# One core, three layers: a GpSimd subtraction cut in four, routed rows fetched two units ahead, first counts a step later

## The chip, the core and the metric

The kernel runs on one core of a Trainium2 chip. The metric is the device time of one execution in microseconds; less is better. TensorE multiplies matrices, VectorE and ScalarE work element by element and can read TensorE's accumulators (PSUM), GpSimd works element by element on SBUF only and issues indirect loads and stores, SyncE issues plain loads and stores.

## The reference, cut to what matters

A gated linear attention (an mLSTM, 4 batches, 8 heads, 768 positions, 40 features), then a dense layer pair with squared ReLU, then a mixture of 8 experts in which each of 3072 tokens goes to the one expert with the largest logit:

```
for t in range(S):                        # attention, per batch and head
    m_new = max(f[t] + m, i[t])
    C = exp(f[t] + m - m_new) * C + exp(i[t] - m_new) * outer(v[t], k[t])
    n = exp(f[t] + m - m_new) * n + exp(i[t] - m_new) * k[t]
    y[t] = sigmoid(o[t]) * (C @ q[t]) / max(abs(n @ q[t]), 1)
g = relu(x @ w_in) ** 2 ; x = g @ w_out   # dense, 320 -> 2048 -> 320
e = argmax(x @ w_gate, axis=1)            # routed, 320 -> 1024 -> 320
out[token] = gate * relu(x[token] @ w1[e]) @ w2[e]
```

All is in float32. The kernel multiplies in a faster format and therefore splits operands in a rounded high part and a low part (the value minus its high part).

## The kernel before, in words

**Attention and dense part.** The 3072 tokens are 24 chunks of 128, and a dense group is 3 chunks (8 groups). While TensorE runs the dense layers of group g, the attention of later chunks is woven in between in small steps; `attend` makes 0.7 half steps for each of a group's 16 pairs of first layer (`l1`, line 802) and second layer (`l2`, line 833). Two first layers run ahead of the second (`AHEAD`). All engines have queues that are worked off in order, in the order in which the program writes them.

From chunk 7 on (`WHOLE`) the operands of the scores are split. `round(j)` (line 614) does this for the keys (j = 0) and the queries (j = 1) of the next chunk: ScalarE writes the scaled and rounded copy into `kq` (line 619), GpSimd subtracts it from `st` in place over 1024 columns (line 620). That is 2 x 17 subtractions. Around them GpSimd adds a bias to the decays `Ab` (line 648), masks them (line 649), and weighs the values (line 664); ScalarE takes the exponential of `Ab` (line 654) after the mask. In the same ScalarE queue stand the activations of the dense layers, `g` and `gh` (lines 821, 822). VectorE then makes `g` squared again and its low part `gl` (lines 828, 829), which the second layer needs.

**A group's end.** `fin(g)` (line 915) is a generator; each `next` on it is one step, and one step is made in each of the following iterations of the second layer. It writes the group's rows, transposes them for the logits `lp`, and then works on VectorE: logits, largest value and its index, the index as a number (`ei`, line 946). For group 0 it also counts the tokens per expert: the one-hot rows `on` (line 950) are summed by three small matmuls `ep` (line 952), and the fullest expert is chosen to be the first one. Then follow the one-hot `oh` (line 967), the softmax's exponent on VectorE and ScalarE (969, 970), and, a step later, the ranks' matmuls `pr` (line 973).

**Routed part.** `routed_experts` has one program for each engine with counting semaphores. A unit is up to 384 tokens of one expert; between 7 and 15 units, all but the first with weights loaded by SyncE, split by ScalarE (high) and by VectorE and GpSimd (low; GpSimd has piece 5). For unit u+1 TensorE transposes the gathered rows (`xT`, line 260) in the middle of unit u, at steps 5 and 6 of its first layer and in its second. It waits there for the indirect loads on `sG`. GpSimd's body for unit t is: gather the rows of unit t+1 (three indirect loads), scatter the results of unit t-1, make low piece 5 of unit t+1, drain. `gather(u)` waits on `sXL` until the rows of unit u-2 are split, since it writes their buffer. Orders of the others that matter are written out:

```
ACT_ORDER = "g0 g1 h0 g2 g3 h1 g4 g5 h2 g6 g7 x0 x1 h3 x2 h4 h5 p0 p1 p2".split()
DVE_ORDER = "g0 g1 l0 g2 g3 l1 g4 g5 l2 g6 g7 x0 x1 l3 x2 l4".split()
```

g: first layer's output; h and l: high and low pieces of the next unit's weights; x: the next unit's rows; p: output.

Of the kernel before, what the change touches and what calls it, by code (L numbers as in the profile page):

```python
# [9 lines left out]
F32 = mybir.dt.float32  # L10
# [8 lines left out]
ALU = mybir.AluOpType  # L19
# [66 lines left out]
def routed_experts(tc, pools, weights, x_d, w12, out, idx, tab, c0, gts, ident):  # L86

    nc = tc.nc
# [7 lines left out]
    op = [ps.tile([128, DM], F32, name=f"op{i}") for i in range(2)]  # L96
# [6 lines left out]
    def cell(e, u, j, lo, hi):  # L103
        return e.value_load(tab[u:u + 1, j:j + 1], min_val=lo, max_val=hi)

    def first_weights(e, load, have):

        with e.If(cell(e, 0, 3, 0, 1) < 1):
            load()
        with e.Else():  # L110
            have()

    def nest(e, body):

        mine = bass.OrderedEngineSet([e.engine])
        name = lambda t, k="": f"{e.engine.name}_unit{t}{k}"
        for t in range(MIN - 1):
            body(t, True)
        n = cell(e, 0, 2, MIN, NU)
        e.br(name(MIN - 1))  # L120
        for t in range(MIN - 1, NU):
            if t < NU - 1:
                with nc.body(name(t), valid_engines=mine):
                    e.br_cond(n > t + 1, name(t, "more"), name(t, "last"))
                with nc.body(name(t, "more"), valid_engines=mine):
                    body(t, True)
                    e.br(name(t + 1))
            with nc.body(name(t, "last" if t < NU - 1 else ""), valid_engines=mine):
                hint = e.mark_branch_hint_location()
                body(t, False)  # L130
                e.br(name(NU)).branch_hint(hint)
        nc.switch_bb(name(NU))
# [17 lines left out]
    def low(e, u, j):  # L150
        e.wait_ge(sH[j], u + 1)
        o = wl[u % 2][0][:, cut[j]] if j < 3 else wl[u % 2][1][:, CUT[j] - W1:CUT[j + 1] - W1]
        e.tensor_tensor(out=o, in0=raw[:, cut[j]], in1=wh[u % 2][:, cut[j]].bitcast(F32), op=ALU.subtract).then_inc(sW[j], 1)

    def pool(e):
        def gather(u):
            if u >= 2:
                e.wait_ge(sXL, 3 * (u - 1))
            for j in range(3):
                i = 3 * (u % 2) + j  # L160
                e.indirect_dma_start(out=xg[u % 2][:, j], out_offset=None, in_=x_d, in_offset=bass.IndirectOffsetOnAxis(ap=idx[:, 3 * u + j:3 * u + j + 1].bitcast(U32), axis=0)).then_inc(sG[i], 16)  # L161

        def put(at, j):
            e.indirect_dma_start(out=out, out_offset=bass.IndirectOffsetOnAxis(ap=at.bitcast(U32), axis=0), in_=ot[j], in_offset=None, bounds_check=NT - 1, oob_is_err=False).then_inc(sO[j], 16)  # L164

        def scatter(u, js=range(3)):
            for j in js:
                e.wait_ge(sOT, 3 * u + j + 1)
                put(idx[:, 3 * u + j:3 * u + j + 1], j)

        def body(t, more):
            if t:
                gather(t + 1)
            if t:
                scatter(t - 1)
            if more:
                for j in POOL_LO:
                    low(e, t + 1, j)
                e.drain()  # L179
            else:  # L180
                c = cell(e, t, 0, 1, GT)
                scatter(t, [0])
                for j in (1, 2):
                    with e.If(c > L * j):
                        scatter(t, [j])
                        e.wait_ge(sO[j], 16 * (t + 2))
                    with e.Else():
                        e.wait_ge(sO[j], 16 * (t + 1))
                e.wait_ge(sO[0], 16 * (t + 2))
        gather(1)  # L190
        for j in range(3):
            put(idx0[:, j:j + 1], j)
        first_weights(e, lambda: [low(e, 0, j) for j in POOL_LO], lambda: [e.sem_inc(sW[j], 1) for j in POOL_LO])
        nest(e, body)

    def act(e):
# [169 lines left out]
def kernel(ctx, tc, qk, q3, kvo, gates, w_in, w_out, wg, w12, cst, out, dbg=None):  # L366
    nc = tc.nc
# [218 lines left out]
    class Chunk:  # L586
# [27 lines left out]
        def round(self, j):  # L614

            if j == 0:
                self.kq = at1.tile([120, 2, H * L], F32R, tag="kq", name="kq")
            o = self.kq[:, j]
            nc.scalar.activation(out=o, in_=self.st[j], func=ACTF.Copy, scale=third[:, j:j + 1])  # L619
            nc.gpsimd.tensor_tensor(out=o, in0=self.st[j], in1=o.bitcast(F32), op=ALU.subtract)  # L620

        def decays(self):
            self.Ab = []
# [223 lines left out]
    def bc(ap, n):  # L847
        return ap.to_broadcast([ap.shape[0], ap.shape[1], n])

    def row(ap, n):  # L850
        return ap.rearrange("p (o e) -> p o e", o=1).to_broadcast([ap.shape[0], n, ap.shape[1]])
# [35 lines left out]
    def counts(p, start, stop, *parts):  # L887

        for i, (cols, x) in enumerate(parts):
            nc.tensor.matmul(p[:, cols].rearrange("p t e -> p (t e)"), ones, x.rearrange("p t e -> p (t e)"), start=start and i == 0, stop=stop and i == len(parts) - 1)  # L890
# [24 lines left out]
    def fin(g, acc):  # L915
# [31 lines left out]
        if g == 0:  # L947

            on = rw.tile([128, 3, 8], BF16, tag="so", name="on")
            nc.vector.tensor_tensor(out=on, in0=row(io8, n), in1=bc(ei, 8), op=ALU.is_equal)  # L950
            ep = psa.tile([128, 1, 8], F32, tag="a", name="ep")
            counts(ep, True, True, *[(slice(0, 1), on[:, t:t + 1]) for t in range(n)])
            yield
            mc = rw.tile([128, 8], F32, tag="mc", name="mc")
            nc.vector.tensor_copy(out=mc, in_=ep[:, 0])
            mm = rw.tile([128, 8], F32, tag="mm", name="mm")
            nc.vector.max(out=mm, in_=mc)
            mi = rw.tile([128, 8], U32, tag="mi", name="mi")
            nc.vector.max_index(out=mi, in_max=mm, in_values=mc)
            ef = rw.tile([128, 1], F32, tag="ef", name="ef")  # L960
            nc.vector.tensor_copy(out=ef, in_=mi[:, 0:1])
            nc.vector.tensor_copy(out=e0, in_=ef[0:1])
            ri = rw.tile([128, 8], I32, tag="ri", name="ri")
            nc.vector.tensor_tensor(out=ri, in0=io8, in1=ef.to_broadcast([128, 8]), op=ALU.add)
            nc.vector.tensor_scalar(out=ri, in0=ri, scalar1=7, scalar2=None, op0=ALU.bitwise_and)
            nc.vector.tensor_copy(out=rot, in_=ri)
# [156 lines left out]
    with tc.manual_schedule():  # L1123
# [36 lines left out]
        def layer2():  # L1160
# [21 lines left out]
            if f == NF - 1:  # L1182
                if g == NG - 1:
                    for j in range(i - 2, i + 1):
                        l2(g, accs[g], [2], its[j][1], *gs.pop(j))
                q = fin(g, accs.pop(g))
                next(q)
                before = list(fins)
                fins.append(q)
                if g == NG - 2:  # L1190
                    leave(brief)
                    p0 = ctx.enter_context(tc.tile_pool(name="p0", bufs=1, side="right"))
                    w0.extend([p0.tile([128, WN], F32R, name="w0h"), p0.tile([128, W1], F32R, name="w01l")])
                    fins.append(first_unit(before, p0))
                if g == NG - 1:
                    leave(dense)
                    fins[:] = [last_tokens(q)]
# [136 lines left out]
        while nd[0] < len(its):  # L1334
            i = nd[0]
# [126 lines left out]
```

## Time and profile before

| what | us |
|---|---|
| median of 3 runs shown (816.49 to 826.73) | 817.44 |
| the profiled execution | 819.06 |
| its span | 817.3 |
| TensorE busy in it | 761.4 |
| VectorE / ScalarE / GpSimd busy | 532.6 / 434.7 / 356.5 |
| mean granted TensorE clock | 0.978 |

All rows below are of that profiled execution, in microseconds from the start of its span. The engines are PE (TensorE; PEld its weight loads), DVE (VectorE), ACT (ScalarE), POOL (GpSimd), SP (SyncE). The attention runs until about 470 us beside the dense part, the dense part until about 560, and the routed part from about 595 us.

### The profile page before, as it was taken

The numbers are of one execution on the slowest core, as the hardware profiler recorded it, in microseconds if no ns is written. First come the engines' busy times: TensorE is split into PE (matmuls) and PEld (weight loads), VectorE is DVE, ScalarE is ACT, GpSimd is POOL, SyncE is SP. The second block draws the span as 40 slices with busy tenths as digits, with TensorE's granted clock in tenths as the row PEclk, the third lists the DMA queues.
The fourth block names the chain that finished last, engine by engine and source line by source line (L and its number), as shares of the span: only waits on it lengthen the run. The fifth ranks groups of instructions, "written<-read, shape, count | busy, mean of one in ns | idle before, by whom it ended". The sixth has DMA issues, their size and how long they took to land.

```text
span 817.3 us, 14079 instructions
## 1 busy us (share of the span) xinstructions
PE 761.4 (93%) x5075; PEld 745.2 (91%) x5075; DVE 532.6 (65%) x1169; ACT 434.7 (53%) x810; POOL 356.5 (44%) x329
## 2 busy tenths in 40 slices
PE   5779989989989999999999999999989999799995
PEld 3679989989989999989998999999989999699995
DVE  5678787777686787776679755362556546667553
ACT  5788785534544643543454533553256555566553
POOL 3774665535552553463345300423125334556423
PEclk9999999989999999998999999999999999999998
DMA  7777536344834344334335000100167566577602
GB/s 202 191 233 219 162 118 167 110 141 120 250 105 127 111 116 134 107 105 140 107 115 160 8 1 30 32 30 1 60 231 253 173 194 187 185 225 222 193 24 60
DMA packets 58824, 109.30 MB, mean 134 GB/s; under 512 B 7132, under 2 KB 36413, under 8 KB 58614
## 3 DMA queue, kind: packets, MB, share of 16 engines
q1 hardware_dynamic: 49542, 84.67, 35.4%
q0 software_dynamic: 4160, 11.77, 5.0%
q10 hardware_dynamic: 5040, 11.82, 4.9%
q8 instruction: 46, 0.75, 0.4%
q14 instruction: 36, 0.29, 0.1%
HBM read 99.37 MB, written 10.50 MB: 134 GB/s over the span
## 4 chain that ended last, share of the span: by engine, by line
PE 47%; issue 19%; POOL 10%; DVE 8%; DMA 7%; ACT 4%; POOLq 3%; SPq 0%; ACTq 0%; DVEq 0%
PE hp L813 18%; PE acc L842 6%; PE acc L844 5%; PE acc L843 5%; DMA st<-in_qk_dram 5%; POOL out_dram L164 4%; PE pv L748 3%; POOLq L179 3%; PE sp L739 2%; PE tp L704 2%; PE lp L907 2%; POOL kq L620 1%; POOL xrl L161 1%; PE xpt L713 1%; DVE gl L829 1%
## 5 line engine op out<-in xcount | busy, mean ns | idle before, releaser
L842 PE MATMUL acc<-wo_h,gh 128*128 128x320 f32 x384 | 126.1, 328 | 0.0
L821 ACT ACTIVATE g<-hp 128x384 f32<-128x384 f32 x128 | 62.3, 487 | 114.2 <-PE hp L813 109.2
L844 PE MATMUL acc<-wo_h,gl 128*128 128x320 f32 x384 | 120.2, 313 | 0.9 <-DVE gl L829 0.9
L843 PE MATMUL acc<-wo_l,gh 128*128 128x320 f32 x384 | 119.7, 312 | 0.0
L620 POOL TENSOR_TENSOR kq<-st,kq 120x1024 fp32r<-120x1024 f32 x34 | 83.7, 2464 | 81.8 <-ACT kq L619 72.1
L813 PE MATMUL hp<-xh,win_h 128*128 128x384 f32 x384 | 115.1, 354 | 3.7 <-ACT scr L902 1.3
L828 DVE SCALAR_TENSOR_TENSOR g<-hp,g 128x384 f32<-128x384 f32 x128 | 70.3, 549 | 68.2 <-ACT gh L822 68.2
L829 DVE TENSOR_TENSOR gl<-g,gh 128x384 fp32r<-128x384 f32 x128 | 97.0, 758 | 8.2
L249 DVE SCALAR_TENSOR_TENSOR gl<-hp,gh 128x384 fp32r<-128x384 f32 x88 | 47.7, 555 | 78.5 <-ACT gh L219 77.1
L813 PE MATMUL hp<-xh,win_l 128*128 128x384 f32 x384 | 89.1, 340 | 0.0
L813 PE MATMUL hp<-xl,win_h 128*128 128x384 f32 x256 | 88.1, 344 | 0.0
L844 PEld LDWEIGHTS acc<-wo_h,gl 128*128 128x128 f32 x384 | 73.3, 191 | 1.2 <-DVE gl L829 1.2
L842 PEld LDWEIGHTS acc<-wo_h,gh 128*128 128x128 f32 x384 | 73.7, 192 | 0.4
L843 PEld LDWEIGHTS acc<-wo_l,gh 128*128 128x128 f32 x384 | 73.6, 192 | 0.0
L813 PEld LDWEIGHTS hp<-xh,win_h 128*128 128x128 f32 x384 | 66.9, 193 | 5.8 <-DVE Ab L743 2.1
L822 ACT ACTIVATE gh<-g 128x384 fp32r<-128x384 f32 x128 | 67.2, 525 | 8.6 <-PE acc L843 4.6
L813 PEld LDWEIGHTS hp<-xh,win_l 128*128 128x128 f32 x384 | 70.6, 192 | 0.0
L219 ACT ACTIVATE gh<-hp 128x384 fp32r<-128x384 f32 x88 | 42.9, 491 | 50.5 <-PE hp L280 50.0
L619 ACT ACTIVATE kq<-st,cs 120x1024 fp32r<-120x1024 f32 x34 | 39.0, 1146 | 50.6 <-DMA st<-in_qk_dram 44.0
L748 PEld LDWEIGHTS pv<-kvo,Ab 128*128 128x128 f32 x384 | 56.2, 219 | 9.2 <-DVE Ab L743 3.4
L748 PE MATMUL pv<-kvo,Ab 128*128 128x42 f32 x384 | 55.0, 301 | 7.9 <-DVE Ab L743 5.1
L648 POOL TENSOR_TENSOR Ab<-Ab,cT 128x512 f32<-128x512 f32 x46 | 56.2, 1222 | 0.2
(265 smaller groups left out, 1848.7 us busy)
## 6 DMA issues: line engine op xcount, KB each, us to landing
st<-in_qk_dram SPq DMA_DIRECT2D x34, 480.0 KB, 8.1
raw<-in_w_dram SPq DMA_DIRECT2D x30, 512.0 KB, 4.8
kvo<-in_kvo_dram SPq DMA_DIRECT2D x24, 529.0 KB, 6.8
Ab<-A_d SPq DMA_DIRECT2D x46, 256.0 KB, 3.9
raw<-in_w_dram SPq DMA_DIRECT2D x20, 427.0 KB, 3.6
raw<-in_w_in_dram ACTq DMA_DIRECT2D x16, 384.0 KB, 3.5
raw<-in_w_out_dram ACTq DMA_DIRECT2D x16, 320.0 KB, 3.7
raw<-in_w_dram SPq DMA_DIRECT2D x10, 426.0 KB, 3.9
```

Of the source, the lines that this page charges most:

```text
L249: e.scalar_tensor_tensor(out=gl[:, j], in0=hp[j % 4], scalar=0.0, in1=gh[:, j].bitcast(F32), op0=ALU.max, op1=ALU.subtract).then_inc(sGL, 1)
L620: nc.gpsimd.tensor_tensor(out=o, in0=self.st[j], in1=o.bitcast(F32), op=ALU.subtract)
L648: nc.gpsimd.tensor_tensor(out=Ab, in0=Ab, in1=cT[:, self.c, col:col + 7:2].rearrange("p (h o) -> p h o", o=1).to_broadcast([128, 4, L]), o ...
L748: nc.tensor.matmul(pv[:, hd], d.Ab[r][:, i], d.v[:, hd], start=True, stop=True)
L813: nc.tensor.matmul(hp, a, x, start=(n == 0), stop=(n == 7))
L821: nc.scalar.activation(out=r, in_=hp, func=ACTF.Relu)
L822: nc.scalar.activation(out=gh, in_=r, func=ACTF.Square)
L828: nc.vector.scalar_tensor_tensor(out=r, in0=hp, scalar=0.0, in1=r, op0=ALU.max, op1=ALU.mult)
L829: nc.vector.tensor_tensor(out=gl, in0=r, in1=gh.bitcast(F32), op=ALU.subtract)
L842: nc.tensor.matmul(acc[t][:, 0:DM], gh[:, sl], wh, start=(f == 0), stop=False)
L843: nc.tensor.matmul(acc[t][:, 0:DM], gh[:, sl], wl, start=False, stop=False)
L844: nc.tensor.matmul(acc[t][:, 0:DM], gl[:, sl], wh, start=False, stop=end)
```

## The change

Three edits. The subtraction of line 620 is written as four of 256 columns. In the routed part GpSimd's body for unit t gathers the rows of unit t+2 where a unit follows (before: t+1, in every body but the first), and the drain moves from behind the low piece to ahead of it. In `fin(0)` there is one more step between `on` and its counts.

```diff
         def body(t, more):
-            if t:
-                gather(t + 1)
+            if more:
+                gather(t + 2)
             if t:
                 scatter(t - 1)
             if more:
+                e.drain()
                 for j in POOL_LO:
                     low(e, t + 1, j)
-                e.drain()
             else:
...
-            nc.gpsimd.tensor_tensor(out=o, in0=self.st[j], in1=o.bitcast(F32), op=ALU.subtract)
+            for i in range(4):
+                c = slice(256 * i, 256 * i + 256)
+                nc.gpsimd.tensor_tensor(out=o[:, c], in0=self.st[j][:, c], in1=o[:, c].bitcast(F32), op=ALU.subtract)
...
             nc.vector.tensor_tensor(out=on, in0=row(io8, n), in1=bc(ei, 8), op=ALU.is_equal)
+            yield
             ep = psa.tile([128, 1, 8], F32, tag="a", name="ep")
             counts(ep, True, True, *[(slice(0, 1), on[:, t:t + 1]) for t in range(n)])
             yield
```

## Rows read from the trace of the kernel before

**Rows 1.** The page's first part: busy time, share of the span, instructions of each engine.
```profile
PE 761.4 (93%) x5075; PEld 745.2 (91%) x5075; DVE 532.6 (65%) x1169; ACT 434.7 (53%) x810; POOL 356.5 (44%) x329
```

**Rows 2.** Waits, whole span: engine, line <- what released it: us, times, longest.
```profile
ACT Ab L654 <- POOL Ab L649: 45.5, 21, 3.9
...
PE xp L266 <- DMA xrl<-x_d,idx: 5.2, 4, 4.2
...
PE pv L748 <- DVE xh L723: 2.8, 2, 2.4
...
PE ep L890 <- DVE on L950: 2.3, 1, 2.3
PE pr L973 <- DVE xh L723: 2.0, 1, 2.0
...
PE xp L266 <- DMA xr<-x_d,idx: 1.2, 2, 1.0
PE pr L973 <- DVE g L828: 1.1, 1, 1.1
...
PE hp L813 <- ACT gh L822: 1.0, 1, 1.0
```

**Rows 3.** Windows: length, busy (instructions) of PE, PEld, DVE, ACT, POOL, PE's clock, DMA.
```profile
164.00:176.00 12.00, 9.74 (x48) 9.66 (x48) 8.70 (x36) 2.02 (x5) 3.08 (x4) 0.72 0.38 110
236.00:240.00 4.00, 1.65 (x12) 1.36 (x11) 3.25 (x7) 2.05 (x5) 2.42 (x4) 1.00 0.00 0
300.00:304.00 4.00, 2.86 (x28) 2.69 (x26) 3.89 (x9) 2.34 (x5) 2.38 (x5) 1.00 0.00 0
364.00:376.00 12.00, 12.00 (x51) 12.00 (x52) 10.85 (x31) 3.33 (x7) 4.34 (x3) 0.57 0.26 78
704.00:712.00 8.00, 5.54 (x33) 5.25 (x34) 2.19 (x4) 1.76 (x5) 4.71 (x4) 0.79 0.69 240
```

**Rows 4.** Single lines: duration in ns, least/median/most; first and last start; shape.
```profile
L620 POOL TENSOR_TENSOR kq<-st,kq x34: 2375/2397/2736, 128.4 to 457.9; 120x1024 fp32r<-120x1024 f32 x34
...
L568 POOL TENSOR_TENSOR win_l<-raw,win_h x14: 997/1019/1280, 20.6 to 103.7; 128x384 fp32r<-128x384 f32 x14
...
L568 POOL TENSOR_TENSOR wo_l<-raw,wo_h x11: 861/883/1222, 39.3 to 118.0; 128x320 fp32r<-128x320 f32 x11
...
L829 DVE TENSOR_TENSOR gl<-g,gh x128: 557/559/2666, 75.1 to 559.6; 128x384 fp32r<-128x384 f32 x128
```

**Rows 5.** Timeline, POOL and DVE around 240 us: start, duration, engine, line, operation.
```profile
240.03 2.40 POOL L620 TENSOR_TENSOR kq<-st,kq 120x1024 fp32r<-120x1024 f32 x1 [1.54 <-ACT kq L619]
242.39 1.36 POOL L648 TENSOR_TENSOR Ab<-Ab,cT 128x512 f32<-128x512 f32 x1
...
240.54 2.31 DVE L829 TENSOR_TENSOR gl<-g,gh 128x384 fp32r<-128x384 f32 x1
```

**Rows 6.** Timeline, DVE and POOL around 360 us (the end of a group).
```profile
359.18 1.93 DVE L946 CAST ei<-ix 128x3 f32<-128x3 uint32 x1
361.15 0.98 DVE L967 TENSOR_TENSOR oh<-rot,ei 128x24 bf16<-128x24 f32 x1
...
358.65 2.38 POOL L620 TENSOR_TENSOR kq<-st,kq 120x1024 fp32r<-120x1024 f32 x1 [2.13 <-ACT kq L619]
361.04 1.05 POOL L648 TENSOR_TENSOR Ab<-Ab,cT 128x512 f32<-128x512 f32 x1
```

**Rows 7.** Timeline, DVE around the first group's counts.
```profile
165.35 0.98 DVE L950 TENSOR_TENSOR on<-cs,ei 128x24 bf16<-128x24 f32 x1
167.99 0.56 DVE L829 TENSOR_TENSOR gl<-g,gh 128x384 fp32r<-128x384 f32 x1
```

**Rows 8.** Timeline, routed part: GpSimd's late gather, and TensorE's transposes that wait.
```profile
700.08 1.53 POOL L161 DMA_INDIRECT xrl<-x_d,idx  x1 [1.31 <-issue]
...
705.96 0.55 PE L266 MATMUL xp<-cs,xrl 128*128 128x128 f32 x3 [4.21 <-DMA xrl<-x_d,idx]
...
802.52 0.55 PE L266 MATMUL xp<-cs,xr 128*128 128x128 f32 x3 [1.00 <-DMA xr<-x_d,idx]
```

## What I predict, with its working

> **What bounds the kernel now.** I read the busy times first. TensorE is busy for 761 us of a span of 817 [rows 1], so the kernel is TensorE's time, its pauses, and the stretches in which it is granted the lower of its two clocks. GpSimd, at 44%, has room in total. Second came the list of waits, read for TensorE first [rows 2]. Four causes stand out that the change touches: 6.4 us for gathered rows in the routed part (5.2 and 1.2), 2.3 us for the first group's counts, and three waits (2.4, 2.0 and 1.1, the first being the longest of a row of 2.8) in which VectorE comes late with a group's routing. Third came windows around those places, for the clock [rows 3]. After the counts' wait the clock is 0.72 of full speed over 12 us: 12 x 0.28 = 3.4 us lost. After the 2.0 us wait at 361 us it is 0.57 over 12 us: 5.2 us lost. Around the longest gather wait it is 0.79 over 8 us; weighted with the 5.5 us in which TensorE worked, 1.2 us. These are stretches that mix 2.4 with 1.2 GHz. But a pause does not always cost the clock: the windows at 236 and 300 us hold pauses of 2.35 and 1.14 us and stay at 1.00.
>
> **The four pieces.** Today one subtraction of 1024 columns takes 2397 ns, 34 times [rows 4]. The only rows of the same operation at two smaller sizes, in SBUF and mostly undisturbed, are 1019 ns for 384 columns and 883 ns for 320 [rows 4]: 2.125 ns a column and 203 ns fixed. A piece of 256 columns is then 747 ns and four are 2.99 us. Neighbours on GpSimd overlap by 0.04 us (240.03 + 2.40 against 242.39, [rows 5]), so I take 2.99 - 0.12 - 2.40 = 0.47 us more for each, 16 us of GpSimd in all. Bounds: 0 if the time is proportional to the columns, 0.59 without overlap, so 0 to 20 us.
>
> The Trainium skill (GPSIMD Engine Reference, section 3.1) gives 4497 ns for 2048 columns of such an operation. An estimate from this page's figure and the 2397 ns row puts the fixed part at 297 ns, a piece at 822 ns, and the addition at 0.77 us each after the same overlap, 26 us in all; by the page the pieces speak more against themselves than by the rows, and no run here has the page's size.
>
> What the pieces buy is VectorE's. The `gl` subtraction takes 557 ns alone and up to 2666 [rows 4]; the one that starts at 240.54 ends at 242.85, just after GpSimd's at 242.43, and GpSimd's next operation, which usually takes 1.05 us, is stretched to 1.36 [rows 5, 6]. So a held VectorE operation gets in at the end of GpSimd's instruction even when another is queued behind. With pieces it should be held 0.75 us at most. At 359.18 the `ei` cast is held to 361.1 by the subtraction that began at 358.65, and `oh` to 362.1 by the next operation [rows 6]. With pieces the cast goes at 359.40, `oh` behind the second piece at about 360.3, and the operation after it about 361.1, where today it can only follow 362.1. I take 1.0 us off each of the three waits: 3.0 us (bounds 0, if something else ends the wait, and all 5.5). The pause at 361 us then is 1.0 us, nearest to that of the 300 us window, which kept its clock. So I take the 5.2 us back as well.
>
> Against it: after the second subtraction of a chunk, GpSimd's bias addition and mask follow, and ScalarE stands in its queue on that mask, 45.5 us in 21 waits, 2.2 us each [rows 2]. Behind it are the `g` and `gh` activations that TensorE's second layer needs two steps later. Two subtractions lengthened by 0.47 us, each stretched by one more VectorE operation by 0.3 us (the 1.36 against 1.05, [rows 5, 6]), make the mask 1 to 2 us late. Of today's 21 waits TensorE sees one of 1.0 us (`hp` on `gh`, [rows 2]); the rest is hidden by the two units of first layer that run ahead. Bounds: nothing, or 1.5 us in each of 17 chunks, 25 us. It is nearest to hidden; I charge four such waits of 1.0 us, 4.0 us.
>
> **The counts a step on.** The extra `yield` moves the three small matmuls and everything behind them one second-layer iteration later. `on` ends at 166.33 [rows 7], and TensorE now reaches the counts after another iteration, so their 2.3 us wait goes. What is late next is VectorE: its C update, `g` and `gl` still follow `on`, and this `gl` ends at 168.55 [rows 7], while TensorE, 2.3 us ahead and at full clock, would ask for it earlier. Bounds for that new wait: 0 and 2.3; I take half, 1.1. Gain 1.2 us, and with a pause of 1.1 us the 3.4 us of low clock too. The later expert choice is covered: its weights are asked for a whole group later.
>
> **The gathers.** `gather(t+2)` in body t goes out about one routed unit earlier. No DMA is added: three indirect loads a unit, and the three of the last unit disappear from its body, because they went out in the body before. They pass three things in GpSimd's queue: the `low` piece, the drain, and the scatter of the unit before. The new wait is for the same unit's split columns (`sXL`); by the written-out orders those end before the last high piece of the weights, on which GpSimd stands anyway, so the scatters behind it are not delayed. The drain now stands ahead of `low`, which waits for ScalarE in any case. In the longest case the gather was issued at 700.08, its first issue alone took 1.53 us, and TensorE waited 4.21 us; in the last unit it waited 1.00 us for rows that nobody computes on [rows 8]. All 6.4 us go and the 1.2 us of clock: 7.6 us. Bounds: 5.2 (4.21 + 1.00 alone), if a wait for weights takes the place of the small ones, and 7.6.
>
> **Sum.** 7.6 + 1.2 + 3.4 + 3.0 + 5.2 = 20.4. Two corrections. Where the clock stays up, VectorE's backlog is met sooner: from 364 to 376 us it was busy 10.85 of 12 us [rows 3] while TensorE crept; I charge a wait of 1.1 us, like the row of that size, at each of the two places, 2.2. And 4.0 for ScalarE. Left: 14.2 us. The profiled execution took 819.06 us (its span plus 1.8), so 804.9. It stands 1.62 above the median shown, 817.44, so I forecast **803.2** there.
>
> **Rivals.** (1) *More.* ScalarE's lateness and the backlog are hidden and the counts' wait has no successor: 14.2 + 4.0 + 2.2 + 1.1 = 21.5, 795.9. For it: TensorE sees one of 21 ScalarE waits today. Against: VectorE is busy nearly all the time after a group's end. (2) *The clock falls all the same.* Both low stretches stay, without the backlog: 14.2 - 3.4 - 5.2 + 2.2 = 7.8, 809.6. For it: it followed pauses of 2.0 and 2.3, and a remnant may be enough. Against: the 300 us window. (3) *Slower: the mask decides.* GpSimd, interrupted at each piece, brings the mask late by 1.5 us in all 17 chunks and all of it reaches TensorE: 18.2 gained without my 4.0, 25.5 lost, 824.7. It decides from 18.2 / 17 = 1.07 us per chunk that TensorE sees. For it: ScalarE's queue is in order and 21 waits are there already. Against: the one row of 1.0. The Trainium skill (SBUF — State Buffer, "Who interferes with whom") says that whichever of VectorE and GpSimd issues first has the shared ports for its whole instruction and the other blocks fully; by that, each gap between pieces is an invitation to VectorE, and the 1.36 us row agrees. (4) *The pieces do nothing.* Back to back they keep VectorE out as one instruction does: no 3.0, no 5.2, one backlog charge less, 817.44 - 14.2 + 8.2 - 1.1 = 810.3. Against: VectorE got in between two queued GpSimd instructions [rows 5].
>
> **Chances and range.** Forecast case, 799 to 807: 0.50. More: 0.23. Clock falls: 0.17. Slower: 0.05. Pieces idle: 0.05. The range that leaves out no more than two in ten is 795 to 811; the forecast's own is 799 to 807. 2% is 16.3 us, about what a measurement of this kernel can tell from no change: 801.1 and 833.8. Below 801.1 lie rival 1 and a quarter of the forecast case: 0.36. Above 833.8 lies only the worst of rival 3, with low clock on top: 0.03. Within: 0.61.
>
> **What would show it.** Gathers: no TensorE wait of `xp` on a DMA, and full clock from 700 to 712 us. Pieces: 136 instructions of about 0.72 us, `gl` at most about 1.35 us, casts near 0.8 us; TensorE's waits behind VectorE near 1 us, and 364 to 376 us at full clock. Counts: no wait of `ep`; a shorter one on `gl` soon after. Rival 3 shows as ScalarE's waits on the mask far above 45 us with TensorE waits on `gh`. I am wrong if the pieces hold the ports together, if a pause of 1 us drops the clock, or if another lateness appears at each group's end.

## The result, and the profile after

The changed kernel took 807.68 us (median; before beside it 817.09), a ratio of 0.986 with a 95% interval of 0.981 to 0.991: 9.4 us faster by the medians, inside the range on record, 4.5 us above the forecast and just above the forecast's own 799 to 807. Its profiled execution has a span of 806.1 us. The whole change was timed twice more, on two chips, each time beside the kernel before; which chip the first comparison ran on is not known:

| comparison | before | after | ratio | 95% interval |
|---|---|---|---|---|
| first comparison | 817.09 | 807.68 | 0.986 | 0.981 to 0.991 |
| chip of e1 to e4 | 813.56 | 796.44 | 0.979 | 0.971 to 0.987 |
| chip of e9 to e12 | 817.10 | 805.72 | 0.989 | 0.984 to 0.994 |

So the gain is 9 to 17 us by medians; the intervals overlap, so the times alone don't show that it depends on the chip. Here are TensorE's longest waits in the kernel after, in the first comparison (engine, line, what released it: us in total, times, longest):

```profile
PE hp L280 <- issue: 5.7, 4, 3.7
PE Ap L639 <- DMA cs<-in_cst_dram: 5.7, 1, 5.7
PE pv L750 <- DVE Ab L745: 4.6, 2, 3.1
```

No wait of `xp` for gathered rows is left (6.4 us, [rows 2]), nor the wait of `ep`. At the top stands something new: 5.7 us, "issue" (the profile shows nothing that TensorE waited for), at the first layer of the routed part. The windows show what went with the waits (length, busy time of PE, PEld, DVE, ACT, POOL, PE's clock, DMA):

```profile
164.00:176.00 12.00, 11.30 (x79) 10.65 (x79) 11.31 (x40) 5.01 (x11) 4.83 (x9) 1.00 0.68 188
352.00:364.00 12.00, 11.25 (x85) 10.93 (x83) 10.94 (x34) 5.99 (x12) 7.56 (x11) 1.00 0.26 81
364.00:376.00 12.00, 11.77 (x77) 11.48 (x76) 7.28 (x12) 4.78 (x9) 5.81 (x7) 1.00 0.56 157
412.00:420.00 8.00, 8.00 (x34) 7.96 (x34) 4.57 (x20) 3.38 (x7) 1.51 (x2) 0.57 0.07 20
592.00:604.00 12.00, 8.27 (x44) 7.90 (x43) 5.40 (x11) 5.28 (x10) 3.06 (x4) 0.72 0.90 338
704.00:712.00 8.00, 8.00 (x61) 8.00 (x62) 4.58 (x9) 5.19 (x9) 3.63 (x4) 1.00 0.74 219
```

All three stretches that were at 0.72, 0.57 and 0.79 before [rows 3] are at full clock. Two new low ones stand at 412 (after a pause of 1.39 us behind VectorE) and at 592, where TensorE worked 8.3 of 12 us.

Because single executions differ, I compare stretches of all the profiled executions, each cut at the starts of the same three instructions of VectorE: a `gl` near 129 us, the row index (`idx`, at 567 to 585 us), and the third `gl` of the routed part. What lies before the first mark varied by up to 7.6 us between executions with no order in it, and is left out. The lengths in us, read from the timelines:

| kernel | attention and dense, to the row index | start of the routed part | rest, to the end |
|---|---|---|---|
| before | 455.3 | 17.6 | 215.2 |
| before, again (e8) | 447.8 | 17.7 | 215.5 |
| gathers alone (e2) | 452.0 | 17.6 | 207.0 |
| counts alone (e3) | 455.7 | 17.2 | 214.0 |
| pieces alone (e1) | 444.0 | 16.6 | 214.5 |
| pieces and gathers (e5) | 446.5 | 16.6 | 206.2 |
| whole, two pieces (e6, e10) | 444.4, 445.2 | 16.4, 23.4 | 206.0, 208.9 |
| whole, eight pieces (e7) | 449.5 | 17.4 | 205.9 |
| whole change: first comparison, e4, e9 | 444.5, 439.8, 440.3 | 23.6, 16.6, 23.8 | 209.4, 205.6, 206.8 |
| whole, drain behind `low` (e11) | 441.8 | 23.5 | 211.4 |
| whole, bias cut too (e12) | 442.8 | 22.7 | 209.9 |

Read by columns: the pieces act in the first (the counts alone don't show there), the gathers in the last, and the middle one holds a stall of 6 to 7 us (with its low clock) that comes or stays away.

### The profile page after: what moved, and what is told of

It is laid out like the page before. It is cut to its first block, busy times and chain, and to the rows that moved or that the text cites. A ratio compares the mean times of both kernels' runs of the same rounds, so it can differ in the third digit from the quotient of the medians.

```text
span 806.1 us, 14205 instructions
## 1 busy us (share of the span) xinstructions
PE 758.2 (94%) x5075; PEld 742.0 (92%) x5075; DVE 521.2 (65%) x1169; ACT 433.8 (54%) x810; POOL 372.5 (46%) x431
## 4 chain that ended last, share of the span: by engine, by line
PE 62%; DVE 11%; DMA 8%; POOL 6%; ACT 6%; issue 6%; SPq 0%; ACTq 0%; POOLq 0%; DVEq 0%
PE hp L815 15%; PE hp L280 13%; DMA st<-in_qk_dram 7%; PE acc L844 5%; PE acc L846 5%; PE acc L845 4%; POOL kq L622 4%; PE op L300 3%; PE op L299 3%; PE op L301 3%; PE pv L750 3%; PE tp L706 2%; ACT raw L534 1%; PE xp L266 1%; PE sp L741 1%
## 5 line engine op out<-in xcount | busy, mean ns | idle before, releaser
L622 POOL TENSOR_TENSOR kq<-st,kq 120x256 fp32r<-120x256 f32 x136 | 103.2, 789 | 69.5 <-ACT kq L619 66.3
L831 DVE TENSOR_TENSOR gl<-g,gh 128x384 fp32r<-128x384 f32 x128 | 86.6, 676 | 8.3
L656 ACT ACTIVATE Ab<-Ab 128x512 f32<-128x512 f32 x46 | 28.9, 629 | 60.0 <-POOL Ab L651 60.0
L750 PEld LDWEIGHTS pv<-kvo,Ab 128*128 128x128 f32 x384 | 54.4, 213 | 6.0 <-DVE Ab L745 3.3
L750 PE MATMUL pv<-kvo,Ab 128*128 128x42 f32 x384 | 53.0, 294 | 5.3 <-DVE Ab L745 4.6
```

Source lines behind the costliest of these rows:

```text
L622: nc.gpsimd.tensor_tensor(out=o[:, c], in0=self.st[j][:, c], in1=o[:, c].bitcast(F32), op=ALU.subtract)
L750: nc.tensor.matmul(pv[:, hd], d.Ab[r][:, i], d.v[:, hd], start=True, stop=True)
L831: nc.vector.tensor_tensor(out=gl, in0=r, in1=gh.bitcast(F32), op=ALU.subtract)
```

## The experiments

All kernels start from the kernel before or from the changed one; each has the edit shown.

### The three parts alone, and the whole once more (one chip, 813.56 us before)

**e1: the four pieces alone.**

```
+            for i in range(4):
+                c = slice(256 * i, 256 * i + 256)
+                nc.gpsimd.tensor_tensor(out=o[:, c], in0=self.st[j][:, c], in1=o[:, c].bitcast(F32), op=ALU.subtract)
```

> Only the four pieces of GpSimd's subtraction; gathers and counts as before. The step on record (3.0 us of VectorE lateness and 5.2 of low clock after 361 us, minus 4.0 for ScalarE and 1.1 of backlog): 3.1 us faster, about 814. If the low clock is won and ScalarE's lateness stays hidden, as the trace of the changed kernel reads (waits at 236, 256 and 361 us shorter by 1.7, 0.4 and 1.3 us, 5.2 us of clock): 8.6 us faster, about 808.5. If the pieces do nothing by themselves and the counts' step made the whole gain of the attention part: 817, with the 2 us waits at 236 and 361 us still there.

805.03 us, ratio 0.990 (0.986 to 0.993): 8.5 us faster, the second of the three cases. The end of the group that had the 2.04 us wait [rows 2, 6] now reads like this (timeline of e1; start, duration, engine, line, operation):

```profile
348.85 2.82 POOL L622 TENSOR_TENSOR kq<-st,kq 120x256 fp32r<-120x256 f32 x4 [1.64 <-ACT kq L619]
...
349.90 0.41 DVE L948 CAST ei<-ix 128x3 f32<-128x3 uint32 x1
350.34 0.67 DVE L969 TENSOR_TENSOR oh<-rot,ei 128x24 bf16<-128x24 f32 x1
350.93 0.78 DVE L971 TENSOR_TENSOR ex<-lg,mx 128x24 f32<-128x24 f32 x1
...
353.16 0.19 PE L975 MATMUL pr<-oh,tri 128*128 128x24 bf16 x1 [0.78 <-DVE xh L725]
```

The cast, held for 1.93 us before, takes 0.41; `oh` and `ex` each pass while GpSimd is between two pieces, and all three are through at 351.7, 1.8 us after the cast began; before, `oh` alone ended 3.0 us after that start. TensorE's wait behind them is 0.78.

**e2: the gathers alone.**

```
-            if t:
-                gather(t + 1)
+            if more:
+                gather(t + 2)
...
+                e.drain()
                 for j in POOL_LO:
                     low(e, t + 1, j)
-                e.drain()
```

> Only the earlier gathers and the drain ahead of the low piece. The step on record: 6.4 us of waits and 1.2 of clock, 7.6 us faster, about 809.5; the routed part (from the first row-index ready to the end) takes 7.6 us less than before. Rival, that the earlier gather of unit 2 fills the DMA queues and so brings the stall of 3.7 us with its low clock that stands at the start of the changed kernel's routed part: the stall is here too, and the kernel gains nothing, 815 to 819. If the stall is here but the time is won elsewhere, about 812.

804.68 us, ratio 0.986 (0.976 to 0.995), so 4 to 19 us faster. The profiled execution lies 6 us above the median; by stretches it is clear: the rest of the routed part takes 207.0 us, against 214.0 to 215.5 in the four executions with the old gathers. No wait for gathered rows is left, and around the place of the 4.21 us wait TensorE is full:

```profile
696.00:712.00 16.00, 16.00 (x127) 15.99 (x127) 11.90 (x21) 11.68 (x21) 10.84 (x7) 1.00 0.86 266
```

The stall at the start of the routed part is not here.

**e3: the counts alone.**

```
+            yield
             ep = psa.tile([128, 1, 8], F32, tag="a", name="ep")
```

> Only the counts one step on. The step on record: 1.2 us of wait and 3.4 of clock minus 1.1 of backlog, 3.5 us faster, about 813.6, with 164 to 176 us at full clock. If the second subtraction in one piece makes VectorE late there anyway: a new wait of about 2 us within 10 us behind the counts, and no gain, 816 to 817.

810.16 us, ratio 0.998 (0.993 to 1.002): nothing that can be told from no change. The wait of `ep` is gone and 164 to 176 us are at full clock, but a new wait follows, and the clock falls behind it, and again at 232 us, where the kernel before had waited without that loss (windows, then TensorE's row in the timeline):

```profile
164.00:176.00 12.00, 11.34 (x85) 10.91 (x84) 11.41 (x31) 6.19 (x12) 4.07 (x5) 1.00 0.60 168
176.00:180.00 4.00, 1.93 (x8) 1.82 (x7) 3.85 (x8) 0.44 (x1) 3.93 (x4) 0.79 0.00 0
232.00:248.00 16.00, 13.71 (x78) 13.41 (x78) 14.06 (x35) 6.05 (x13) 7.62 (x7) 0.79 0.18 43
```
```profile
178.21 0.88 PE L813 MATMUL hp<-xh,win_h 128*128 128x384 f32 x2 [2.07 <-DVE xh L723]
```

GpSimd and VectorE are busy for 3.9 of the 4 us around it: VectorE's backlog behind a whole subtraction of 1024 columns, met earlier, as the second case said.

**e4: the whole change again.**

> The changed kernel once more beside its three parts on the same chip. If the three parts add up, its gain is the sum of the three. If the stall of ScalarE and TensorE at the start of the routed part (3.66 us at 597 us) belongs to the code, it stands in this profile at the same place with nearly the same length; if it is a fluctuation of one execution, it is gone or elsewhere, and the time is some 7 us lower.

796.44 us, ratio 0.979 (0.971 to 0.987): 17.1 us. The three parts alone make 8.5 + 8.9 + 3.4 = 20.8 by medians, the sum within their intervals. The stall is not there; ScalarE's products follow each other every 0.95 us (shown below), and the windows are full:

```profile
164.00:176.00 12.00, 12.00 (x88) 11.84 (x89) 10.98 (x32) 4.49 (x9) 6.91 (x10) 1.00 0.55 129
352.00:376.00 24.00, 23.72 (x164) 23.16 (x164) 19.08 (x55) 10.47 (x20) 15.05 (x20) 1.00 0.42 120
584.00:596.00 12.00, 12.00 (x92) 11.99 (x92) 7.54 (x14) 6.75 (x13) 7.63 (x8) 0.92 0.94 324
```

### The number of pieces, the counts on top of them, and the kernel before once more (one chip, 816.36 us before)

**e5: pieces and gathers, no extra `yield`.** The edits of e1 and e2 together.

> The four pieces and the earlier gathers, the counts where they were before. If the counts' step adds to the other two (the step on record: 1.2 us of wait and 3.4 of clock less 1.1): 3.5 us slower than the whole change, some 1.7% faster than before. If the counts' step gives back behind it what it wins, as its run alone looked like (3.3 us won at 166 to 178 us, all of it gone by 256): as fast as the whole change, 2.1% faster than before. The wait of ep on VectorE's on, 2.2 us, is back in both.

800.06 us, ratio 0.977 (0.969 to 0.984). By time it can't be told from the whole change. By the trace the wait of `ep` (2.2 us) and the low clock behind it are back, as in every profiled execution without the extra `yield`, and the first column is 2 to 7 us longer than in the three of the whole change:

```profile
164.00:176.00 12.00, 10.15 (x50) 10.14 (x50) 9.72 (x38) 2.67 (x7) 3.46 (x6) 0.72 0.41 123
```

**e6 and e7: two pieces of 512 and eight of 128 columns.**

```
-            for i in range(4):
-                c = slice(256 * i, 256 * i + 256)
+            for i in range(2):
+                c = slice(512 * i, 512 * i + 512)
```

In e7 the range is 8 and the width 128.

> The whole change, but GpSimd's subtraction in two pieces of 512 columns instead of four. From the rows of before (203 ns fixed, 2.125 ns a column) a piece takes 1.25 to 1.29 us, and a subtraction 0.15 us more than in one. If VectorE gets in at the end of each piece, it is held up to 1.3 us instead of 0.75: the VectorE operation behind the expert index ends up to 0.5 us later than with four pieces, TensorE's waits behind VectorE stand between those of before (2.0 to 2.4) and those with four pieces (0.7), and the kernel is 1 to 3 us slower than with four pieces. If what counts is the added GpSimd time, it is as fast or 1 to 3 us faster, since the mask then comes 0.4 us earlier per subtraction. If the pieces' cut does nothing: as with one piece, 8 us slower than four.

> The whole change, but the subtraction in eight pieces of 128 columns. A piece takes 0.44 to 0.48 us by the same rows, a subtraction 3.5 to 3.8 us, 1.1 to 1.4 more than in one piece, so the mask of each chunk is 2.2 us or more later than before. The rival on record that the mask decides puts the point at 1.07 us per chunk that TensorE sees: ScalarE's waits on the mask rise from 60 to 75 us or more, and if TensorE sees them, the gain of the attention part is gone, 816. If ScalarE's lateness stays hidden as with four pieces: within 3 us of the whole change.

e6: 800.25 us, ratio 0.978 (0.972 to 0.985). e7: 804.12 us, ratio 0.983 (0.977 to 0.990). The subtraction's rows (least, median and most ns) in e6, the changed kernel and e7:

```profile
L622 POOL TENSOR_TENSOR kq<-st,kq x68: 1267/1291/1665, 127.3 to 447.0; 120x512 fp32r<-120x512 f32 x68
```
```profile
L622 POOL TENSOR_TENSOR kq<-st,kq x136: 719/737/1068, 127.8 to 448.6; 120x256 fp32r<-120x256 f32 x136
```
```profile
L622 POOL TENSOR_TENSOR kq<-st,kq x272: 446/462/837, 126.7 to 453.5; 120x128 fp32r<-120x128 f32 x136
```

and ScalarE's waits on the mask, in the same order:

```profile
ACT Ab L656 <- POOL Ab L651: 48.4, 22, 4.2
```
```profile
ACT Ab L656 <- POOL Ab L651: 60.0, 24, 4.3
```
```profile
ACT Ab L656 <- POOL Ab L651: 74.7, 24, 4.9
```

With the 2397 ns of one piece [rows 4], four sizes lie on one line: 186 ns fixed and 2.16 ns a column. ScalarE's waits on the mask rise with the number of pieces, 48.4, 60.0, 74.7 us, and the wait of TensorE's first layer (`hp`) on ScalarE's `gh` [rows 2] is in none of the three. With two pieces TensorE's longest wait of `hp` on VectorE's `xh` is 2.1 us (1.3 in e10), with four 0.5 to 0.7. With eight pieces the attention part takes 449.5 us, 5 to 10 more than with four, and what TensorE waits for most there is VectorE (`hp` on `g`, two waits, the longest 1.9). The timings of two, four and eight pieces don't separate them (four with the extra `yield` were not timed on this chip); e7's attention part is one execution.

**e8: the kernel before, unchanged.**

> The kernel before, unchanged, profiled once more: how much of what its first trace showed is chance. If the low clock behind the pauses at 164 and 361 us belongs to these pauses, it stands at the same two places, 6.8 and 10.2 us long, and the waits of 2.3, 2.4 and 2.0 us too. If a pause of that size only sometimes costs the clock, the waits are the same and the low stretches are elsewhere or fewer, and the time differs by 3 to 5 us for each. The first 128 us may differ by up to 4 us in any case, as they did between the five traces so far.

815.44 us against 816.36, ratio 1.001 (0.997 to 1.005). Its profiled execution has a span of 809.4 us, 8 less than the first one shown. The counts' wait (2.3) and the low clock behind it are the same. The wait at the end of the later group is nearly the same, but the clock behind it stays up (TensorE's row and the windows of e8):

```profile
359.23 0.19 PE L973 MATMUL pr<-oh,tri 128*128 128x24 bf16 x1 [1.93 <-DVE xh L723]
```
```profile
236.00:240.00 4.00, 4.00 (x36) 4.00 (x35) 3.93 (x6) 1.68 (x4) 3.93 (x3) 1.00 0.22 66
356.00:368.00 12.00, 10.07 (x74) 9.74 (x73) 10.98 (x29) 5.98 (x12) 6.62 (x7) 1.00 0.24 67
364.00:376.00 12.00, 11.88 (x80) 11.56 (x80) 9.74 (x32) 5.52 (x10) 2.94 (x3) 1.00 0.79 225
```

The 2.35 us wait at 236 is not there either. So the 5.2 us of low clock that I charged to the wait at 361 us don't come with it each time: a pause of 1.93 us cost nothing here, one of 2.04 cost 12 us at 0.57.

### A third chip (817.10 us before): the stall, the drain, the bias

**e9: the whole change a third time.**

> The whole change a third time, to size it: the first chip gave 1.4% with a stall of 3.7 us in the profiled execution, the second 2.1% without. If the stall is a chance of single executions, this profile is without it as the second was, and the gain is 2%; if it comes back at the start of the routed part, the gain is 1.4% and the change has a cost there.

805.72 us, ratio 0.989 (0.984 to 0.994), and the stall is back at the same place with the same length. ScalarE's timeline in e9, and the same stretch in e4 below it ("remote": no instruction in the profile released it):

```profile
583.45 0.49 ACT L219 ACTIVATE gh<-hp 128x384 fp32r<-128x384 f32 x1 [2.04 <-PE hp L280]
587.02 0.49 ACT L219 ACTIVATE gh<-hp 128x384 fp32r<-128x384 f32 x1 [3.08 <-PE hp L280]
592.74 0.49 ACT L219 ACTIVATE gh<-hp 128x384 fp32r<-128x384 f32 x1 [5.22 <-remote]
594.23 1.25 ACT L219 ACTIVATE gh<-hp 128x384 fp32r<-128x384 f32 x3 [1.00 <-remote]
```
```profile
586.47 0.49 ACT L219 ACTIVATE gh<-hp 128x384 fp32r<-128x384 f32 x1 [0.91 <-PE hp L280]
587.41 0.49 ACT L219 ACTIVATE gh<-hp 128x384 fp32r<-128x384 f32 x1 [0.45 <-PE hp L280]
588.36 0.49 ACT L219 ACTIVATE gh<-hp 128x384 fp32r<-128x384 f32 x1 [0.45 <-PE hp L280]
```

and what GpSimd and TensorE do in e9 meanwhile (timeline; the `xrl` load is the first of unit 2, which the change moved here):

```profile
589.03 0.99 POOL L161 DMA_INDIRECT xrl<-x_d,idx  x1 [0.30 <-issue]
...
593.87 0.58 PE L280 MATMUL hp<-xh,w0h 128*128 128x256 f32 x1 [3.74 <-issue]
```

TensorE's second product was complete at about 584.4 and the third at 585.3, but ScalarE rounded the second at 587.02 and the third at 592.74. So ScalarE was 2.6 us late before the moved loads were issued at 589.03, and was then idle for 5.2 us with its input ready. TensorE, which runs four products ahead, stopped for 3.74 us. SyncE is late as well, and earlier. Its first six weight loads of the routed part, in e9 and then in e4:

```profile
585.55 5.71 SPq L139 DMA_DIRECT2D raw<-in_w_dram  x6
```
```profile
584.13 3.52 SPq L139 DMA_DIRECT2D raw<-in_w_dram  x6
```

Counted from the row index, the first goes out after 16.0 us in e9 and 12.8 us in e4. In the five profiled executions with the stall it goes out after 15.0 to 16.6 us and the six take 5.4 to 5.7 us; in the nine without it after 12.6 to 14.6 us, and they take 3.1 to 3.9 us. Later in the stretch the DMA queues are as full in e4 (329 and 364 GB/s from 586 to 594 us) as in e9 (321 and 375), without a stall in e4.

**e10: two pieces again, beside four.** The edit of e6.

> The whole change with two pieces of 512 columns once more, beside four pieces on the same chip. If the length for which VectorE is held is what the pieces buy: 1 to 3 us slower than four pieces. If the GpSimd time added is what they cost (0.5 us less per subtraction, mask waits of ScalarE 48 us instead of 60): 1 to 3 us faster. If both are small against what is left: within 2 us.

807.06 us, ratio 0.984 (0.977 to 0.991), against 805.72 with four: not separated. The stall is there too (`hp` on "issue", longest 3.7 us).

**e11: the drain back behind the low piece.**

```
-                e.drain()
                 for j in POOL_LO:
                     low(e, t + 1, j)
+                e.drain()
```

> The whole change with GpSimd's drain left behind its low piece, as before. The step on record: the drain's place costs nothing once the rows go out two units ahead, as fast as the whole change within 2 us, and no wait of TensorE for gathered rows. If the gain of the routed part came from the drain's place (the gather then follows the low piece at 0.15 us instead of 3.5): the wait of xp for gathered rows is back, and the kernel is 6 us slower.

804.69 us, ratio 0.987 (0.981 to 0.992): as the whole change. GpSimd's next gather follows its low piece with 1.3 us or more of idle time again, and TensorE has no wait of `xp` on a DMA: that these waits are gone is the earlier gather's doing, not the drain's. The last stretch, 211.4 us, is the longest of the five with the stall, so a small share of the drain is not excluded.

**e12: the bias addition in two pieces.**

```
-                nc.gpsimd.tensor_tensor(out=Ab, in0=Ab, in1=cT[...].to_broadcast([128, 4, L]), op=ALU.add)
+                for h in (0, 2):
+                    nc.gpsimd.tensor_tensor(out=Ab[:, h:h + 2], in0=Ab[:, h:h + 2], in1=cT[...].to_broadcast([128, 2, L]), op=ALU.add)
```

> The whole change, and GpSimd's bias addition (512 columns, 1.05 us) cut in two pieces of 256 as well. If VectorE's holds still set TensorE's waits, the remaining stretch of VectorE behind this addition (up to 0.8 us, 4 to 5 us in all between 128 and 474 us) halves and the kernel gains 1 to 3 us. If the cut costs (about 0.15 us of GpSimd on each of 46 additions, ahead of the mask on which ScalarE stands): 0 to 3 us slower.

803.57 us, ratio 0.985 (0.980 to 0.990), against 805.72: not separated, and the attention part, 442.8 us, is not shorter than with the change alone (439.8 to 444.5). So cutting this addition does not shorten the waits behind VectorE that are left.

## Why the prediction was right, step by step

The total was right, but in part because two errors stood against each other in the first comparison. The attention part gained 10.8 us between the two profiled executions, where I forecast 6.6. In the routed part the last stretch gained 5.8 us and the stretch with the stall lost 6.0, where I forecast a gain of 7.6. That these two nearly cancel is luck.

**Gathers: right, and a little small.** 7.6 us forecast. With the four old-gather executions at 214.0 to 215.5 us (mean 214.8) and the five new ones without the stall at 205.6 to 207.0 (mean 206.1), the rest of the routed part is 8.7 us shorter. The full clock around 704 to 712 us and the missing `xp` waits are as listed. By e11 it is the earlier gather that removes the waits.

**Counts: the step right, its surroundings mis-sized.** Up to 176 us, e3 did what the sum says: no 2.3 us wait, full clock. The step that failed is "0 and 2.3; I take half, 1.1" for what is late next. Alone, it was nearly the upper bound (2.07), and the clock fell behind it and again in the window from 232 us. With the pieces it was smaller (0.21 and 0.71 at 175 and 176 us in the changed kernel), which fits a shorter backlog of VectorE. The two edits seem to belong together: three executions with both average 441.5 us in the attention part, the two with the pieces but the old counts 445.2, counts alone 455.7. The first two differ by less than single executions of one kernel do, so this is not shown by time; what the profiles show is the low clock behind the counts, 6.8 us in each of the five without the extra `yield` and at most 3.4 with it.

**Pieces: the durations right, the price wrong.** The working from two other rows gave 747 ns a piece, and 737 was measured; the added 0.47 us was 0.42 for the four in a row shown for e1 (2.82 us) and, with VectorE's turns in it, 0.57 in the mean of all in the changed kernel (103.2 us in 34 subtractions, against 83.7). The 1.0 us off each wait was a little small: 2.04 became 0.75 in the changed kernel, and 2.35 became 0.69. The longest `gl` went from 2666 to 1450 ns, where I said 1350. VectorE does get in after each piece, so rival 4 falls. The Trainium skill (SBUF — State Buffer, "Who interferes with whom") has the first issuer hold the shared ports for one instruction; the `ei` row, 1.93 us behind a whole subtraction and 0.41 behind a piece, agrees. The estimate from the Trainium skill (GPSIMD Engine Reference, section 3.1), 297 ns fixed, was too dear: the runs give 186. One reading was wrong: the bias addition does not usually take 1.05 us in the kernel before. Of its 32 rows behind 128 us 18 take 1.35 us or more, in the changed kernel 2, which fits VectorE's turns having moved from it to the pieces.

**ScalarE: the step that failed.** I charged 4.0 us for a later mask. The mask is later (60.0 us of waits instead of 45.5), but TensorE's one wait on that `gh` is gone in the changed kernel, and with eight pieces, at 74.7 us, there is none either. All of TensorE's waits on ScalarE between the first two marks come to 1.9 us in the changed kernel and 1.8 with eight pieces, where they were 2.3 before. It should have been 0, the bound that I named "nearest" and then left. Rival 3 falls with it: at eight pieces the subtraction takes 8 x 0.46 = 3.7 us, two of them 2.6 us more in a chunk, far beyond its 1.07, and the kernel is still 1.7% faster than before.

**The clock behind the 361 us wait: right in part by luck.** I took back 5.2 us as if they belonged to the pause. In e8 the unchanged kernel didn't lose them, and e2, with whole subtractions and a 1.52 us pause, didn't either; e3 did (0.68 from 360 to 376 us, as before). Of the ten executions with pieces none lost them. So the loss came in two of the four with whole subtractions, and the kernel before that I read happened to be one of them. That none of the ten has it fits the shorter pause; four executions are few to show it.

**What the sum missed.** The sum on record for the attention part is 1.2 + 3.4 + 3.0 + 5.2 - 2.2 - 4.0 = 6.6; without this clock, its backlog charge and ScalarE's 4.0 it is 6.6 - 5.2 + 1.1 + 4.0 = 6.5. The two executions of the kernel before average 451.6, those of the whole change 441.5: about 10 us, so the sum was too small. e1 alone, 8.5 us against a sum of 3.1, says the same of the pieces. The profiles divide the 10 us. These are the windows of this stretch in the two executions of the kernel before, then in the three of the whole change (the first two numbers behind the window are its length and TensorE's busy time):

```profile
129.15:584.49 455.34, 440.53 (x3037) 434.69 (x3036) 308.82 (x763) 210.89 (x402) 181.73 (x156) 0.98 0.34 98
128.36:576.16 447.80, 436.57 (x3038) 430.10 (x3038) 307.03 (x763) 210.67 (x402) 181.70 (x156) 0.99 0.35 100
```
```profile
128.57:573.11 444.54, 435.85 (x3037) 429.89 (x3037) 299.30 (x762) 210.15 (x402) 199.09 (x258) 0.99 0.34 100
131.60:571.36 439.76, 432.62 (x3038) 426.70 (x3038) 299.58 (x762) 209.62 (x402) 199.28 (x258) 1.00 0.35 101
129.19:569.51 440.32, 432.45 (x3037) 426.77 (x3037) 298.22 (x762) 209.56 (x402) 198.84 (x257) 1.00 0.35 101
```

TensorE is idle for 14.8 and 11.2 us before, and for 8.7, 7.1 and 7.9 after. By the traces' clock records it is at the lower of its two clock levels for 17.9 and 6.8 us before, and for 7.5, 0 and 0 after; at half the clock, half of such time is lost. Busy time less this half is 431 to 433 us in all fourteen executions, so idle time and clock account for the differences in length. On average the waits give 5.1 us and the clock 4.9. The sum had the waits 2.0 us longer (1.2 + 3.0 - 2.2 - 4.0) and 8.6 us back from the clock (3.4 + 5.2): the two charges, for ScalarE and for the backlog, were the larger error, and the clock hid part of it.

**The stall: not foreseen.** It takes 6 to 7 us in the middle column and up to 5 more behind it. It is in the five profiled executions with the new gathers from the first comparison and from the chip of e9 to e12. It is in none of the five on the chips of e1 to e4 and of e5 to e8, nor in any of the four with the old gathers (none of those was profiled on the chip of e9 to e12). Its size would be enough for the spread between 9 and 17 us. Its cause stays open, and chip and change are not told apart. That SyncE and ScalarE are late before the moved loads go out speaks against these loads; the kernel before on the chip of e9 to e12, at 817.10 us about as slow as elsewhere (813.56 and 816.36), gives no sign of a stall of its own, which speaks weakly for a part of the change. ScalarE idles with its inputs ready, as it would if its next instructions were late; that is argued, not shown. The Trainium skill (Runtime: NRT & Kernel Launch, "Instruction fetch mechanics") says that an engine's instructions come by DMA in blocks and that a jump outside the loaded ones stalls it. The traces list such loads, in DMA queues named "instruction", and speak against it: in none of the five does one run while ScalarE stands idle for these 5 us. In e9 the last before it starts at 583.85 us and the next at 597.57; in e4, without the stall, they start at 584.65 and 593.61. A run of the kernel before and of the gathers alone on the chip of e9 to e12, profiled, would tell chip and change apart.

## What to carry to other kernels

Where a long instruction of an engine off the critical path holds another engine up, cut it: the cost is its fixed part (186 ns here) per cut, and the gain is the other engine's longest hold. Two, four and eight pieces could not be told apart by time; in the attention part of the whole change TensorE was idle for 7.1 to 8.8 us with four, 10.2 and 10.6 with two and 12.1 with eight. Before charging a low clock to a pause, look at a second execution of the same kernel: the pause at 361 us recurred without the low clock, and the one at 236 us, 2.35 us long, was down to 0.21. Sum idle time and lower clock by stretch before dividing a gain. And compare executions in stretches cut at the same instructions, not by totals, when the total varies by 10 us and the change is worth that much.

## What the hardware showed that I had not expected

- GpSimd's subtraction of two SBUF operands follows one line from 128 to 1024 columns: 462, 737, 1291 and 2397 ns. The bias addition (one operand broadcast) has another slope and nearly the same fixed part: 1050 ns at 512 columns (e9), 618 at 256 (e12), so 1.69 ns a column and 186 ns.
- The same pause, 1.93 or 2.04 us at the same place of the same program, left the granted clock at 1.00 in one execution and at 0.57 over the next 12 us in another.
- ScalarE stood idle for 5.2 to 5.7 us with its input ready, and SyncE's six loads took 5.4 to 5.7 us instead of 3.1 to 3.9, in all five profiled executions with the new gathers from the first comparison and from the chip of e9 to e12, in none of five on the two other chips.
